# Depthwise-separable 1x1 convolution: the weight load in two parts, the first input chunk on a second queue, fewer filler matmuls, and the last wait moved to GpSimd

One core of one Trainium2 chip. The metric is the device time of one execution in microseconds (us), as the median of repeated runs; the kernel before takes 574.88 us (three runs, 574.85 to 574.94).

## The reference

```python
H = W = 384; C = 384; k = 1            # x: (1, 384, 384, 384), dw: (1, 1, 384), pw: (384, 384), bf16
out = x * dw[0, 0]                     # k = 1: the depthwise step is a scale per channel
return jnp.einsum('bhwc,cd->bhwd', out, pw)
```

So it is one matrix product of 147456 rows with a 384x384 matrix, whose row c is scaled by dw[c] first.

## The kernel before

The rows are worked in 288 supertiles of 512 rows. Each is loaded by SyncE, transposed by VectorE in two halves (32x32 blocks, into T), multiplied on TensorE in 48 small matmuls (four at a time, each on a quarter of the array's rows), copied out of PSUM by ScalarE and stored by SyncE. The first chunks of the input are small (1, 1, 2, 2, 4 supertiles, then 10 each): I call them x0 to x4. Each supertile waits for both halves of its T in turn, so it can start once the first half is there. Before the loop the scaled weights w_r are built: TensorE multiplies pw by scaled selection matrices, and ScalarE (five copies) and VectorE (one) bring the result to SBUF. TensorE runs filler matmuls on constants meanwhile, and repeats some build matmuls, to keep its clock up. "Lands" means that all of a load's data has arrived and its semaphore says so.

The loads at the start, and SyncE's last wait:

```python
        nc.scalar.dma_start(dw_row[:], dw.rearrange("a e c -> a (e c)")).then_inc(s_dw, 16)
        nc.sync.dma_start(pw_n[:], pw.rearrange("(k p) d -> p k d", p=P)).then_inc(s_pw, 16)
        load_x(0)
        # ... the list of further loads and stores, in order of need
        for _, f, a in sorted(todo, key=lambda a: a[0]):
            if f is store and a[0] == 0:

                for _ in range(28):
                    nc.sync.wait_ge(s_pw, 16)
            f(*a)
        for o in range(NR):
            n = sum(n_parts[t] for t, c in enumerate(chunks) if c[0] % NR == o)
            nc.sync.wait_ge(s_o[o], 16 * n)
```

The first part of TensorE's program (cut):

```python
        idle_work(4)

        nc.tensor.wait_ge(s_dw, 16)
        for k in range(3):
            mm = nc.tensor.matmul(
                PS[1][:, 0, D + k : D + k + 1],
                lhsT=dw_row[:, P * k : P * k + P],
                rhs=ones[0:1, 0:1],
                start=True,
                stop=True,
            )
        mm.then_inc(s_df)
        idle_work(4)
        nc.tensor.wait_ge(s_pw, 16)
        times = {(1, 1): 3, (2, 0): 2}
        for k in range(3):
            nc.tensor.wait_ge(s_sw, k + 1)
            for r in range(2):
                if k == 2:
                    nc.tensor.wait_ge(*w_done[r])

                for v in [0, 1] * times.get((k, r), 1):
                    mm = nc.tensor.matmul(
                        PS[(k + 1) % 2][:, 2 * r + v, :D],
                        lhsT=sel_w[64 * v : 64 * v + 64, k, r, :, :].rearrange("p q w -> p (q w)"),
                        rhs=pw_n[64 * v : 64 * v + 64, k, :],
                        start=True,
                        stop=True,
                        tile_position=(64 * v, 0),
                    )
```

The supertile (cut), with the blocks b of 64 input channels in order 0 to 5:

```python
        steps = [(b, par) for b in range(4) for par in range(2)] + [(4, 0), (5, 0), (4, 1), (5, 1)]
        # per step and quarter q: wait for T's half at b = 0 and b = 3, a matmul into PS[s][:, q],
        # and at ((2, 1), (5, 1)) a semaphore that lets VectorE overwrite that half of T
```

ScalarE's and VectorE's copies of the built weights:

```python
        def w_out(i):
            e, k, r = w_eng[i], i // 2, i % 2
            out, in_ = w_r[:, 2 * k : 2 * k + 2, r, :], w_ps(i)
            o = nc.vector.tensor_copy(out, in_) if e == 0 else nc.scalar.copy(out, in_)
            o._wait_ge(s_w, i + 1)
            o.then_inc(s_wr[e])
```

## Time and profile before

| | before |
|---|---|
| time, median | 574.88 us (574.85 to 574.94) |
| span of the profiled run | 573.1 us |
| TensorE, loop matmuls | 561.8 us busy, 0.2 us idle |
| first build matmul / first loop matmul | 3.98 / 7.06 us |
| last stores landed | 572.0 us |

By this reading only what lies before 7.06 and behind the last matmul (568.85) can change with such an edit. The prediction below shows the lines and how to read them.

### The profile page before, as it was taken

How to read it: one execution, taken by the hardware profiler on the slowest of the kernel's cores; microseconds unless marked ns; L12 is line 12 of the kernel's file. 1: busy time of each engine (PE TensorE's matmuls, PEld its weight loads, DVE VectorE, ACT ScalarE, POOL GpSimd, SP SyncE). 2: the span in 40 equal slices, each digit the busy share in tenths (PEclk: the TensorE clock that was granted, in tenths of full speed). 3: DMA queues.
4: the chain of work that ended last, by engine and by line, in shares of the span. 5: the costliest groups of instructions: out<-in, count | busy, mean ns of one | idle time of the engine just before them, and what ended most of it. 6: DMA issues, size and time to landing. Idle time of an engine off the chain costs nothing.

```text
span 573.1 us, 29723 instructions
## 1 busy us (share of the span) xinstructions
PE 567.5 (99%) x13877; PEld 415.5 (72%) x13877; DVE 507.7 (89%) x584; ACT 419.4 (73%) x297; POOL 0.5 (0%) x5
## 2 busy tenths in 40 slices
PE   9999999999999999999999999999999999999996
PEld 5777777777777777777777777777777777777774
DVE  7888898898898899889889889988988988988995
ACT  6777777777777777777777777777777777777775
POOL 0000000000000000000000000000000000000000
PEclk9999999999999999999999999999999999999999
DMA  8999999999999999999999999999999999999676
GB/s 332 430 350 437 418 422 434 442 415 424 428 421 419 381 400 434 398 381 400 427 390 394 392 427 392 414 402 429 390 399 430 397 393 399 424 398 380 263 286 245
DMA packets 26452, 226.88 MB, mean 396 GB/s; under 512 B 1225, under 2 KB 6986, under 8 KB 22602
## 3 DMA queue, kind: packets, MB, share of 16 engines
q1 hardware_dynamic: 25408, 226.01, 97.3%
q10 hardware_dynamic: 1034, 0.79, 0.4%
q14 instruction: 9, 0.07, 0.0%
q8 instruction: 1, 0.02, 0.0%
HBM read 113.54 MB, written 113.25 MB: 396 GB/s over the span
## 4 chain that ended last, share of the span: by engine, by line
PE 98%; DMA 0%; ACT 0%; issue 0%; DVE 0%; DVEq 0%
PE ps L191 97%; PE ps L208 0%; DMA out_dram<-O 0%; PE ps L239 0%; ACT O L326 0%; ACT w_r L289 0%; DVE O L324 0%; DVEq L102 0%; PE ps L221 0%
## 5 line engine op out<-in xcount | busy, mean ns | idle before, releaser
L191 PE MATMUL ps<-w_r,T 32*128 32x384 bf16 x13824 | 561.8, 321 | 0.2 <-ACT w_r L289 0.2
L276 DVE STREAM_TRANSPOSE T<-X 128x384 uint32<-128x384 uint32 x572 | 500.9, 878 | 55.3 <-DMA X<-in_x_dram 0.8
L191 PEld LDWEIGHTS ps<-w_r,T 32*128 32x128 bf16 x13824 | 413.1, 93 | 149.1 <-issue 0.7
L326 ACT CAST O<-ps 128x1536 bf16<-128x1536 f32 x287 | 413.3, 1440 | 146.8 <-PE ps L191 146.8
L289 ACT CAST w_r<-ps 128x768 bf16<-128x768 f32 x5 | 3.7, 805 | 1.5 <-PE ps L239 1.4
L208 PE MATMUL ps<-const-bfloat16-1.0 32*128 32x384 bf16 x32 | 2.8, 516 | 1.1 <-PEq L348 1.1
L276 DVE STREAM_TRANSPOSE T<-Xl 128x384 uint32<-128x384 uint32 x4 | 3.5, 878 | 0.4
L324 DVE CAST O<-ps 128x384 bf16<-128x384 f32 x2 | 1.0, 553 | 3.1 <-DMA out_dram<-O 3.1
L239 PE MATMUL ps<-pw_n,sel_w 64*128 64x384 bf16 x18 | 2.9, 507 | 0.0
L239 PEld LDWEIGHTS ps<-pw_n,sel_w 64*128 64x128 bf16 x18 | 1.2, 139 | 1.9 <-issue 1.2
L264 ACT ACT_TABLE_LOAD x1 | 1.3, 1283 | 1.5 <-POOLq L102 1.5
L208 PEld LDWEIGHTS ps<-const-bfloat16-1.0 32*128 32x128 bf16 x32 | 1.1, 124 | 1.6 <-issue 1.4
L289 DVE CAST w_r<-ps 128x768 bf16<-128x768 f32 x1 | 1.0, 958 | 1.1 <-PE ps L239 1.1
L294 DVE TENSOR_REDUCE sel<-eye 128x64 f32<-128x128 bf16 x1 | 0.3, 289 | 1.5 <-POOL eye L254 1.5
L323 ACT CAST O<-ps 128x384 bf16<-128x384 f32 x2 | 0.9, 482 | 0.5 <-PE ps L191 0.5
L301 DVE COPY dw_f<-ps 128x3 f32<-128x3 f32 x1 | 0.2, 161 | 0.9 <-PE ps L221 0.9
L304 DVE TENSOR_SCALAR sel_w<-sel,dw_f 128x256 bf16<-128x256 f32 x3 | 0.9, 349 | 0.0
L221 PEld LDWEIGHTS ps<-const-bfloat16-1.0,dw_row 1*128 1x128 bf16 x3 | 0.3, 115 | 0.4 <-DMA dw_row<-in_dw_dram 0.4
L264 ACT COPY warm<-const-float32-0.0 128x1 f32<-128x1 f32 x2 | 0.3, 190 | 0.0
L254 POOL TENSOR_SCALAR_AFFINE_SELECT eye<-const-bfloat16-1.0 128x128 bf16<-128x128 bf16 x1 | 0.3, 294 | 0.6 <-POOLq L102 0.6
L221 PE MATMUL ps<-const-bfloat16-1.0,dw_row 1*128 1x1 bf16 x3 | 0.3, 176 | 0.0
L348 POOL MEMSET const-uint8-127<- 128x1 uint8 x1 | 0.1, 103 | 0.0
(3 smaller groups left out, 0.3 us busy)
## 6 DMA issues: line engine op xcount, KB each, us to landing
X<-in_x_dram SPq DMA_DIRECT2D x26, 3840.0 KB, 21.9
out_dram<-O SPq DMA_DIRECT2D x26, 3840.0 KB, 27.7
X<-in_x_dram SPq DMA_DIRECT2D x3, 1536.0 KB, 17.8
out_dram<-O SPq DMA_DIRECT2D x4, 768.0 KB, 9.5
out_dram<-O SPq DMA_DIRECT2D x2, 1536.0 KB, 15.1
X<-in_x_dram SPq DMA_DIRECT2D x3, 768.0 KB, 8.1
X<-in_x_dram SPq DMA_DIRECT2D x1, 2304.0 KB, 19.4
out_dram<-O SPq DMA_DIRECT2D x1, 2304.0 KB, 11.2
```

Source lines behind the costliest of these rows:

```text
L191: mm = nc.tensor.matmul(PS[s][:, q, :D], lhsT=Ts[s][32 * q : 32 * q + 32, b, par::2], rhs=w_r[32 * q : 32 * q + 32, b, par, :], start=(b, ...
L208: nc.tensor.matmul(PS[0][:, 2 * (i % 2) + i // 2, :D], lhsT=ones[32 * i : 32 * i + 32, 0:P], rhs=ones[32 * i : 32 * i + 32, :], start=True ...
L221: mm = nc.tensor.matmul(PS[1][:, 0, D + k : D + k + 1], lhsT=dw_row[:, P * k : P * k + P], rhs=ones[0:1, 0:1], start=True, stop=True,)
L239: mm = nc.tensor.matmul(PS[(k + 1) % 2][:, 2 * r + v, :D], lhsT=sel_w[64 * v : 64 * v + 64, k, r, :, :].rearrange("p q w -> p (q w)"), rhs ...
L254: nc.gpsimd.affine_select(out=eye[:], in_=ones[:, 0:P], pattern=[[-1, P]], compare_op=mybir.AluOpType.is_equal, fill=0.0, base=0, channel_ ...
L264: nc.scalar.copy(warm[:, s : s + 1], nc.const_aps.tensor(0.0, [P, 1], F32)).then_inc(s_a[s])
L276: ins = nc.vector.transpose(out=Tw[:, 3 * h : 3 * h + 3], in_=Xw[:, :, j, 96 * h : 96 * h + 96].rearrange("p k (b w) -> p b k w", w=32),)
L289: o = nc.vector.tensor_copy(out, in_) if e == 0 else nc.scalar.copy(out, in_)
L304: nc.vector.tensor_scalar_mul(sel_w[:, k], sel[:].unsqueeze(2).to_broadcast([P, 2, 4, 32]), dw_f[:, k : k + 1]).then_inc(s_sw)
L323: nc.scalar.copy(Ov[:, q, j, :], PS[s][:, q, :D]).then_inc(s_a[s])
L324: nc.vector.tensor_copy(Ov[:, q + 1, j, :], PS[s][:, q + 1, :D]).then_inc(s_d)
L326: a = nc.scalar.copy(Ov[:, :, j, :], PS[s][:, :, :D])
```

## The change

Its intent is to start the loop sooner. The first two thirds of pw come in one load with runs of 1536 bytes instead of 768, which puts even rows of pw in one slot and odd rows in the next; so the selection matrices, the dw slices and the copies go by the parity of the row (blocks 0 and 2, then 1 and 3), and the loop takes its blocks in the order 0, 2, 1, 3. The last third is a second load. x0 goes out on ScalarE's queue. Eight fillers fewer stand before the build, and the repeated build matmuls move from the second step to the third. The wait for the last stores passes from SyncE to GpSimd.

```diff
--- before.py
+++ after.py
@@ -68,7 +68,7 @@
 
     pw_n = consts.tile([P, 3, D], BF16, name="pw_n")
     eye = consts.tile([P, P], BF16, name="eye")
-    sel = consts.tile([P, 2, 32], F32, name="sel")
+    sel = consts.tile([P, 2, 2, 32], F32, name="sel")
     sel_w = consts.tile([P, 3, 2, 4, 32], BF16, name="sel_w")
     w_r = consts.tile([P, NB, 2, D], BF16, name="w_r")
     dw_row = consts.tile([1, C], BF16, name="dw_row")
@@ -92,6 +92,7 @@
     s_o = [nc.alloc_semaphore(f"s_o{i}") for i in range(NR)]
     s_dw = nc.alloc_semaphore("s_dw")
     s_pw = nc.alloc_semaphore("s_pw")
+    s_pw2 = nc.alloc_semaphore("s_pw2")
     s_df = nc.alloc_semaphore("s_df")
     s_sw = nc.alloc_semaphore("s_sw")
     s_dwf = nc.alloc_semaphore("s_dwf")
@@ -146,8 +147,12 @@
 
 
         nc.scalar.dma_start(dw_row[:], dw.rearrange("a e c -> a (e c)")).then_inc(s_dw, 16)
-        nc.sync.dma_start(pw_n[:], pw.rearrange("(k p) d -> p k d", p=P)).then_inc(s_pw, 16)
-        load_x(0)
+        load_x(0, nc.scalar)
+        nc.sync.dma_start(
+            pw_n[:, 0:2].rearrange("p t d -> p (t d)"),
+            pw[0 : 2 * P, :].rearrange("(p t) d -> p (t d)", t=2),
+        ).then_inc(s_pw, 16)
+        nc.sync.dma_start(pw_n[:, 2], pw[2 * P : C, :]).then_inc(s_pw2, 16)
 
         todo = []
         for t, (g, i, off, first, L) in enumerate(chunks):
@@ -161,9 +166,6 @@
                 for _ in range(28):
                     nc.sync.wait_ge(s_pw, 16)
             f(*a)
-        for o in range(NR):
-            n = sum(n_parts[t] for t, c in enumerate(chunks) if c[0] % NR == o)
-            nc.sync.wait_ge(s_o[o], 16 * n)
 
 
 
@@ -178,7 +180,7 @@
             return PS[0 if i in (2, 3) else 1][:, 2 * (i % 2) : 2 * (i % 2) + 2, :D]
 
 
-        steps = [(b, par) for b in range(4) for par in range(2)] + [(4, 0), (5, 0), (4, 1), (5, 1)]
+        steps = [(b, par) for b in (0, 2, 1, 3) for par in range(2)] + [(4, 0), (5, 0), (4, 1), (5, 1)]
 
         def supertile(s, rv):
             for b, par in steps:
@@ -198,7 +200,7 @@
                     )
                     if (b, par) == steps[0] and q == 0:
                         mm._wait_ge(s_a[s], rv)
-                    if (b, par) in ((2, 1), (5, 1)) and q == 3:
+                    if (b, par) in ((1, 1), (5, 1)) and q == 3:
                         mm.then_inc(s_pe)
 
 
@@ -220,26 +222,30 @@
         for k in range(3):
             mm = nc.tensor.matmul(
                 PS[1][:, 0, D + k : D + k + 1],
-                lhsT=dw_row[:, P * k : P * k + P],
+                lhsT=dw_row[:, 2 * P :] if k == 2 else dw_row[:, k : 2 * P : 2],
                 rhs=ones[0:1, 0:1],
                 start=True,
                 stop=True,
             )
         mm.then_inc(s_df)
-        idle_work(4)
+        idle_work(2)
         nc.tensor.wait_ge(s_pw, 16)
-        times = {(1, 1): 3, (2, 0): 2}
+        times = {(2, 0): 3, (2, 1): 2}
         for k in range(3):
-            nc.tensor.wait_ge(s_sw, k + 1)
             for r in range(2):
+                if k == 0:
+                    nc.tensor.wait_ge(s_sw, r + 1)
                 if k == 2:
+                    if r == 0:
+                        nc.tensor.wait_ge(s_pw2, 16)
+                        nc.tensor.wait_ge(s_sw, 3)
                     nc.tensor.wait_ge(*w_done[r])
-
+                slot, h = (r, k) if k < 2 else (2, r)
                 for v in [0, 1] * times.get((k, r), 1):
                     mm = nc.tensor.matmul(
                         PS[(k + 1) % 2][:, 2 * r + v, :D],
-                        lhsT=sel_w[64 * v : 64 * v + 64, k, r, :, :].rearrange("p q w -> p (q w)"),
-                        rhs=pw_n[64 * v : 64 * v + 64, k, :],
+                        lhsT=sel_w[64 * v : 64 * v + 64, slot, h, :, :].rearrange("p q w -> p (q w)"),
+                        rhs=pw_n[64 * v : 64 * v + 64, slot, :],
                         start=True,
                         stop=True,
                         tile_position=(64 * v, 0),
@@ -262,6 +268,10 @@
         ).then_inc(s_sel)
         for s in range(2):
             nc.scalar.copy(warm[:, s : s + 1], nc.const_aps.tensor(0.0, [P, 1], F32)).then_inc(s_a[s])
+
+        for o in sorted(range(NR), key=lambda o: (o - len(groups)) % NR):
+            n = sum(n_parts[t] for t, c in enumerate(chunks) if c[0] % NR == o)
+            nc.gpsimd.wait_ge(s_o[o], 16 * n)
 
         def transposes(t, j):
             g, i, off, first, L = chunks[t]
@@ -285,24 +295,25 @@
 
         def w_out(i):
             e, k, r = w_eng[i], i // 2, i % 2
-            out, in_ = w_r[:, 2 * k : 2 * k + 2, r, :], w_ps(i)
+            out, in_ = (w_r[:, k : k + 3 : 2, r, :] if k < 2 else w_r[:, 4:6, r, :]), w_ps(i)
             o = nc.vector.tensor_copy(out, in_) if e == 0 else nc.scalar.copy(out, in_)
             o._wait_ge(s_w, i + 1)
             o.then_inc(s_wr[e])
 
         nc.vector.wait_ge(s_sel, 1)
-        nc.vector.tensor_reduce(
-            out=sel[:],
-            in_=eye[:].rearrange("p (v w r) -> p r w v", v=2, r=2),
-            op=mybir.AluOpType.add,
-            axis=mybir.AxisListType.X,
-        ).then_inc(s_dwf)
+        for k, split in enumerate(("p (v h w) -> p h w v", "p (v w h) -> p h w v")):
+            nc.vector.tensor_reduce(
+                out=sel[:, k],
+                in_=eye[:].rearrange(split, v=2, h=2),
+                op=mybir.AluOpType.add,
+                axis=mybir.AxisListType.X,
+            ).then_inc(s_dwf)
         nc.vector.wait_ge(s_df, 1)
         nc.vector.tensor_copy(dw_f[:], PS[1][:, 0, D : D + 3]).then_inc(s_dwf)
-        nc.vector.wait_ge(s_dwf, 2)
+        nc.vector.wait_ge(s_dwf, 3)
         for k in range(3):
             nc.vector.tensor_scalar_mul(
-                sel_w[:, k], sel[:].unsqueeze(2).to_broadcast([P, 2, 4, 32]), dw_f[:, k : k + 1]
+                sel_w[:, k], sel[:, k // 2].unsqueeze(2).to_broadcast([P, 2, 4, 32]), dw_f[:, k : k + 1]
             ).then_inc(s_sw)
         for i in range(6):
             w_out(i)
```

## The prediction

> **What bounds the kernel now.** I read the groups of instructions first, then the chain of work that ended last cut to the first 22 us, then the timeline of the same stretch and of the last 7 us, and last the transfers.
>
> Of the groups, one row is the kernel:
>
> ```profile
> L191 PE MATMUL ps<-w_r,T 32*128 32x384 bf16 x13824 | 561.8, 321 | 0.2 <-ACT w_r L289 0.2
> L326 ACT CAST O<-ps 128x1536 bf16<-128x1536 f32 x287 | 413.3, 1440 | 146.8 <-PE ps L191 146.8
> ```
>
> The loop's 13824 matmuls keep TensorE busy 561.8 us with 0.2 us of idle time; ScalarE waits 146.8 us for TensorE, not the other way. They run four at a time: 13824/4 = 3456 rounds, 561.8/3456 = 162.6 ns a round. For 384 columns that is the floor of the warm array (next part). The change touches nothing that the loop repeats: the same 48 matmuls for each of 288 supertiles of 512 rows, in another order of blocks, and the semaphore that frees half of T still fires after the third block. So the 561.8 us stay, and the time is
>
> start of the first loop matmul + 561.8 + what follows the last matmul.
>
> The chain of the head says what sets that start:
>
> ```profile
> 2.63 1.30 PE ps L208 x13
> 3.93 0.04 issue
> 3.98 2.12 PE ps L239 x12
> 6.10 0.02 issue
> 6.12 0.81 ACT w_r L289
> 6.93 0.14 issue
> 7.06 14.94 PE ps L191 x361
> ```
>
> L208 is filler on constants, L239 builds the scaled weights, L289 copies them to SBUF. The chain blames the filler for the start at 3.98. The timeline and the rows of the tile pw_n put another cause beside it:
>
> ```profile
> 0.96 0.43 SPq L149 DMA_DIRECT2D pw_n<-in_pw_dram  x1
> 3.98 2.93 PE L239 MATMUL ps<-pw_n,sel_w 64*128 64x384 bf16 x18
> 4.52 3.80 ACT L289 CAST w_r<-ps 128x768 bf16<-128x768 f32 x5 [1.43 <-PE ps L239]
> DMA to landing us min/median/max: 3.0/3.0/3.0
> ```
>
> pw is issued at 0.96 and lands 3.0 us later, at about 3.95. Filler and pw end together, so only removing both moves the build. From the build's first matmul (call it t0 = 3.98) the rest is fixed work: 0.54 us to ScalarE's first copy (4.52), then copies that stand end to end. The loop needs the first three of ScalarE's: 4.52 + 3 x 0.80 = 6.92, and it starts at 7.06. So **loop start = t0 + 3.08**.
>
> The tail, from the timeline and the queue's waits:
>
> ```profile
> 569.55 0.85 SPq L142 DMA_DIRECT2D out_dram<-O  x2
> SPq L166 <- DMA out_dram<-O: 1.6, 1, 1.6
> ```
>
> The last matmul ends near 568.85, the last stores are issued by 570.40, SyncE waits 1.6 us for them (to 572.0), and the span ends at 573.1: 1.1 us of leaving the program. The time (574.88) is 1.8 us more than the span.
>
> **What the Trainium skill says.**
> 1. "TensorE: Matmul & The Clock Gate", section "Back-to-back issue gap": a warm matmul of N columns follows the last after about N/2.4 + 2.5 ns. For N = 384: 162.5. The trace agrees, 162.6.
> 2. Same page, "Part 1: The HAM clock gate": the array runs at half rate until one activity window of about 3.4 us was busy, and the windows run free. The trace agrees in part. Filler and build matmuls show 516 and 507 ns on average against 321 in the loop; pairs of the build stand 0.32 us apart = 384/1.2. Only the last pair (394 ns, at 6.51) is shortened, so the clock rose at about 6.6 us, just before the loop, although the page's clock row says full throughout. At the end the slice 573.25 to 573.50 shows 0.52 on average, i.e. a drop at about 573.26: 166 windows of 3.413 us (the page's 4096 cycles) back from there is 6.65. Estimate: the deciding window of this run was 3.23 to 6.65.
> 3. "DMA: Bandwidth & Descriptors", section "Queues, rings and completion order": each DMA engine alternates between the issuers' queues packet by packet. "Issuing engines are not separate DMA queues" adds that a second issuer saves issue time only. The trace before has pw and x0 on one queue, so it doesn't show that.
>
> **The change part by part.**
>
> *pw in two loads.* The first is 192 KB in 128 runs of 1536 bytes instead of 288 KB in 384 runs of 768 bytes. The DMA rates in half microseconds before:
>
> ```profile
> 2.00:2.50 0.50, 0.50 (x15) 0.22 (x10) 0.00 (x0) 0.50 (x1) 0.00 (x0) 1.00 0.52 103
> 2.50:3.00 0.50, 0.50 (x15) 0.32 (x11) 0.29 (x2) 0.49 (x3) 0.00 (x0) 1.00 1.05 335
> 3.00:3.50 0.50, 0.50 (x12) 0.22 (x4) 0.50 (x3) 0.09 (x1) 0.00 (x0) 1.00 1.13 421
> ```
>
> The last column is GB/s. pw's 295 kB: 51 by 2.5, 167 more by 3.0, the last 77 at 421 GB/s by 3.18; it counts as landed 0.77 us later. The first load, 197 kB: if it has the engines alone from 2.5 at 335 GB/s, 51 + 146 is there at 2.94, landed at 3.71. If longer runs double the slow start (103 by 2.5, 94 left), 2.78 and 3.55. If x0's transfer, now on another queue and issued at about 1.5 (its data from about 2.55), takes half of the rate from 2.5 on: 51 + 84 by 3.0, 62 left at 210, 3.29, landed 4.06, nothing gained. I take **3.70**, between the first and a mixture of the others: gain 0.25 us.
>
> *Fewer fillers.* Eight matmuls fewer are two rounds of 0.32 us: filler is out of the way by about 3.2 instead of 3.93. Alone worth nothing (pw lands at 3.95); with the earlier pw it lets the build follow it. It leaves TensorE idle some 0.5 us before the build.
>
> *Copies by row parity.* The build computes the same 18 matmuls (2+2+2+2+6+4 against 2+2+2+6+4+2), the six copies keep their sizes and engines, so 3.08 us stay. VectorE makes one more reduction (0.29 us, done by 2.1, beside its wait for dw_f until 2.67): hidden. The scaled selectors end at 3.22, 3.48 and 3.75 as before; the first two are wanted at t0 and t0 + 0.32: not binding. The third build step now waits for the first ScalarE copy (t0 + 1.34), then five pairs of 0.32 end at t0 + 3.0: just not binding. The second part of pw (about 4.4) is wanted at t0 + 1.4 = 5.1.
>
> *x0 on ScalarE's queue.* One more issue of 0.47 us there moves the activation table load (1.28 us) and the two warm copies from 1.51-3.09 to about 2.0-3.6, ahead of the first copy (t0 + 0.54 = 4.3): hidden. x0 landed 3.4 us after its issue (4.9), is first read after VectorE's own copy (5.72 before, 5.45 now): hidden either way.
>
> *GpSimd waits for the stores.* SyncE's wait (to 572.0) passes to GpSimd, which holds the end of the block anyway. SyncE's leaving is then hidden, but GpSimd's leaving, and the other engines' answers to it, now come after the stores. Estimate 0.05 us saved, give or take 0.1.
>
> Sum: head -0.25, tail -0.05, clock +0.1 (next part): 574.88 - 0.2 = 574.7; the likeliest single outcome, without clock trouble, is 574.6.
>
> **The rivals.**
> - *The clock rises late.* With idle time from 3.2 to t0, the window 3.23 to 6.65 is only some 85% busy instead of all but full. The window before it, busy 62% (from 1.12), was not enough. If 85% is not enough either, the clock rises one window later, near 10.06, and 3.3 us of the loop run at half rate: +1.7 us, 576.3. Against it: four timed or profiled runs lie within 0.1 us, so the warming seems to have room. I give it 12%.
> - *x0 steals from pw.* Nothing in the head is gained and t0 stays 3.95 to 4.05: 574.9. For it: the alternation of queues that the skill tells. Against it: pw has half a microsecond of lead. 25%.
> - *The pw load shrinks more than I think*: t0 = 3.45, set then by the second selector (3.48): 574.35. 25%.
> - *Input starvation after an earlier start.* x1 landed at 7.3 and x2 at 9.2. With the loop 0.3 us earlier, supertile 1's second half of T is ready near 8.95 and wanted near 9.7; supertile 2's transposes still start at 9.27, are ready at 11.0 and wanted at 11.7. No loss unless loads slip by 0.7 us.
>
> **Range and chances.** Best case 574.2 (head -0.5, tail -0.15); middle 574.6; no gain 574.9; partly late clock 575.3; a whole window late 576.3 lies outside. Range 574.2 to 575.3. Two per cent is 11.5 us, seven times the worst of these, and head and tail together are only 11 us: within 2% is as good as sure.
>
> **What would show it.** Loop matmuls 321 ns and 561.8 us, with the first at 6.8 (6.6 to 7.1); loop start minus first build matmul 3.08; the first load of pw landed 2.75 us after issue; filler ended by 3.3 and a wait for pw of about 0.4 us; the last landing to the span's end 1.1 us. A late clock would show as loop matmuls of some 500 ns in the first microseconds and 563 us or more of busy time on the loop's row. Wrong would be: a loop row that changes by itself, a start later than 7.1 with full clock, or a time under 574.0 or over 576.5.

## The result

The changed kernel took 575.25 us (median of 6 runs, 574.88 to 575.71), the kernel before 574.80 in the same rounds (6 runs, 574.53 to 574.94). The ratio is 1.0009, with a 95% interval of 0.9996 to 1.0022; ratios here come from the mean times of the fast runs of the same rounds, so they are not quite the ratios of the medians. I had forecast a small gain (574.6); there is none, and the profiled run is 0.3 us longer.

The chain of the head in the changed kernel, to be held against that of before:

```profile
1.87 6.12 DMA X<-in_x_dram
7.99 0.02 issue
8.01 0.87 DVE T L286
8.88 0.14 issue
9.02 12.99 PE ps L193 x313
```

Where the chain of before ran from the build to the loop at 7.06, this one runs through a load of x that is issued at 1.87 and lands at 7.99, and the transpose behind it, and joins TensorE at 9.02. The timeline of the same stretch (columns: start, length, engine, line and operation, count; in brackets the idle time before and what ended it):

```profile
3.58 1.20 PE L245 MATMUL ps<-pw_n,sel_w 64*128 64x384 bf16 x8 [0.29 <-DMA pw_n<-in_pw_dram]
4.13 3.61 ACT L299 CAST w_r<-ps 128x768 bf16<-128x768 f32 x5 [0.61 <-PE ps L245]
6.47 2.13 PE L193 MATMUL ps<-w_r,T 32*128 32x384 bf16 x48 [0.36 <-ACT w_r L299]
8.01 1.56 DVE L286 STREAM_TRANSPOSE T<-X 128x384 uint32<-128x384 uint32 x2 [1.15 <-DMA X<-in_x_dram]
9.02 13.18 PE L193 MATMUL ps<-w_r,T 32*128 32x384 bf16 x320 [0.41 <-DVE T L286]
```

The build starts at 3.58 in place of 3.98, and the loop at 6.47 in place of 7.06: **0.59 us gained**, more than I had forecast. But after one supertile (48 matmuls) the loop stops and goes on at 9.02. In the kernel before, the second supertile started at 9.01: loop start 7.06 and 1.95 us of work. The loop's matmuls themselves cost nearly what they cost before (561.8 us):

```profile
L193 PE MATMUL ps<-w_r,T 32*128 32x384 bf16 x13824 | 562.0, 321 | 0.8 <-DVE T L286 0.4
```

From the second supertile on both run alike, as ScalarE's second and third copies out of PSUM show, first before, then after:

```profile
11.19 1.44 ACT L326 CAST O<-ps 128x1536 bf16<-128x1536 f32 x1 [0.51 <-PE ps L191]
13.14 1.44 ACT L326 CAST O<-ps 128x1536 bf16<-128x1536 f32 x1 [0.51 <-PE ps L191]
```

```profile
11.20 1.44 ACT L337 CAST O<-ps 128x1536 bf16<-128x1536 f32 x1 [1.11 <-PE ps L193]
13.15 1.44 ACT L337 CAST O<-ps 128x1536 bf16<-128x1536 f32 x1 [0.51 <-PE ps L193]
```

(Second supertile start = start of the second copy less 2.18; I use that for the runs below, but for e4, whose second supertile ran at half clock, the timeline.) The chunk that was waited for, x1, took this long from issue to landing, before (issued at 1.97: landed at 7.3) and after (issued at 1.87: landed at 8.0):

```profile
DMA to landing us min/median/max: 5.3/5.3/5.3
```

```profile
DMA to landing us min/median/max: 6.1/6.1/6.1
```

From x1's landing to the second supertile there are 1.03 us (a transpose of 0.87 and two hand-overs). With x1 at 7.3 it could have started at 8.3, and 0.7 us of room were left before. Now x1 comes 0.7 later and the loop 0.6 earlier. The packed trace of the changed kernel says more: x1's semaphore rises in sixteen steps, eleven of them by 6.3 and the last five between 7.7 and 8.0. So the late part of the load, not all of it, sets the 8.0.

The 0.3 us of the span come from the end. The last matmul, the last stores' issue (569.55, two of them over 0.85 us) and the last landing (572.0) stand where they stood. But SyncE's waits at the end read, in the changed kernel:

```profile
SPq L103 <- POOLq L103: 1.9, 1, 1.9
SPq L142 <- ACT O L334: 0.6, 1, 0.6
SPq L370 <- PEq L370: 0.6, 2, 0.4
SPq L370 <- POOLq L103: 0.2, 1, 0.2
```

Before, SyncE waited 1.6 us for the stores itself. Now it waits 1.9 us for GpSimd, which lets it go only after the stores have landed, and 0.2 us once more. From the last landing to the end of the span it is 1.42 us in place of 1.15.

### The profile page after: what moved, and what is told of

Read it like the earlier page. It is cut to its first block, busy times and chain, and to the rows that moved or that the text cites. A ratio compares the mean times of both kernels' runs of the same rounds, so it can differ in the third digit from the quotient of the medians.

```text
span 573.4 us, 29709 instructions
## 1 busy us (share of the span) xinstructions
PE 566.3 (99%) x13869; PEld 420.1 (73%) x13869; DVE 507.6 (89%) x585; ACT 419.0 (73%) x297; POOL 0.5 (0%) x5
## 4 chain that ended last, share of the span: by engine, by line
PE 97%; DMA 2%; DVE 0%; ACT 0%; SPq 0%; issue 0%; POOLq 0%
PE ps L193 97%; DMA X<-in_x_dram 1%; DMA out_dram<-O 0%; ACT O L337 0%; DVE O L335 0%; DVE T L286 0%; SPq L155 0%; SPq L151 0%; SPq L370 0%; POOLq L103 0%; POOLq L359 0%
## 5 line engine op out<-in xcount | busy, mean ns | idle before, releaser
L193 PE MATMUL ps<-w_r,T 32*128 32x384 bf16 x13824 | 562.0, 321 | 0.8 <-DVE T L286 0.4
L193 PEld LDWEIGHTS ps<-w_r,T 32*128 32x128 bf16 x13824 | 418.5, 93 | 144.2 <-issue 1.5
```

What stands on the lines that cost most here:

```text
L193: mm = nc.tensor.matmul(PS[s][:, q, :D], lhsT=Ts[s][32 * q : 32 * q + 32, b, par::2], rhs=w_r[32 * q : 32 * q + 32, b, par, :], start=(b, ...
```

## The experiments

Sixteen runs, in five groups of kernels that shared a chip. S stands for the changed kernel with the wait for the stores put back on SyncE (e1). "Rest" is the time from the last landing to the end of the span. Medians and lowest to highest are of the timed runs; before's median is of the same rounds. There is one profile of each kernel, so its loop start and landings are those of one execution. The diffs below are cut to the lines that matter, and are made on S unless the text says otherwise.

| run | loop starts | x1 landed | 2nd supertile | rest | profiled span | median (range) | before | ratio, 95% interval |
|---|---|---|---|---|---|---|---|---|
| before | 7.06 | 7.3 | 9.01 | 1.15 | 573.1 | | | |
| after | 6.47 | 8.0 | 9.02 | 1.42 | 573.4 | 575.25 (574.88-575.71) | 574.80 | 1.0009, 0.9996-1.0022 |
| e0 after again | 6.81 | 8.0 | 9.04 | 1.42 | 573.4 | 575.25 (574.91-575.94) | 574.87 | 1.0008, 0.9994-1.0022 |
| e1 = S | 6.44 | 8.0 | 8.99 | 1.15 | 573.1 | 574.95 (574.28-576.30) | 574.87 | 1.0008, 0.9994-1.0022 |
| e2 before, GpSimd waits | 6.89 | 7.3 | 8.84 | 1.42 | 573.2 | 575.00 (574.88-575.46) | 574.87 | 1.0003, 0.9990-1.0017 |
| e3 after, x0 on SyncE | 7.49 | 7.5 | 9.44 | 1.42 | 573.8 | 575.30 (575.02-575.77) | 574.87 | 1.0007, 0.9993-1.0021 |
| e4 S, x1 on ScalarE | 6.96 | 11.0 | 12.0 | 1.15 | 577.8 | 579.25 (577.51-580.54) | 574.84 | 1.0074, 1.0059-1.0088 |
| e5 S, old fillers | 6.76 | 7.4 | 8.71 | 1.15 | 572.9 | 575.16 (574.60-575.36) | 574.84 | 1.0005, 0.9992-1.0018 |
| e6 before, x0 on ScalarE | 7.09 | 6.1 | 9.04 | 1.15 | 573.2 | 574.79 (574.58-579.21) | 574.84 | 1.0012, 0.9988-1.0036 |
| e7 S, small load third | 6.36 | 8.7 | 9.70 | 1.15 | 573.8 | 575.60 (574.88-576.00) | 574.84 | 1.0011, 0.9998-1.0024 |
| e8 S, pair on ScalarE | 7.04 | (pair) 6.1 | 8.99 | 1.15 | 573.1 | 574.87 (574.67-575.99) | 574.79 | 1.0006, 0.9993-1.0019 |
| e9 S, pw's rest by GpSimd | 9.69 | 5.6 | 13.5 | 1.2 | 577.8 | 578.42 (577.90-579.51) | 574.79 | 1.0064, 1.0051-1.0077 |
| e10 S, x1 before pw's rest | 8.45 | 6.3 | 11.3 | 1.15 | 575.4 | 576.70 (574.91-579.49) | 574.79 | 1.0032, 1.0011-1.0053 |
| e11 S, pw's rest on ScalarE | 6.42 | 7.4 | 8.45 | 1.15 | 572.6 | 574.99 (574.29-576.16) | 574.75 | 1.0007, 0.9993-1.0021 |
| e12 as e11, pair | 8.98 | (pair) 7.0 | 12.7 | 1.15 | 576.8 | 577.21 (575.11-578.50) | 574.75 | 1.0030, 1.0016-1.0044 |
| e13 S, x0 twice (wrong) | 6.68 | 7.7, not waited for | 8.63 | 1.15 | 573.2 | 574.87 (574.78-576.70) | 574.75 | 1.0012, 0.9996-1.0027 |
| e14 before, repeats late | 6.75 | 7.8 | 8.85 | 1.15 | 573.0 | 574.72 (574.46-574.88) | 574.85 | 0.9998, 0.9984-1.0011 |
| e15 = e11 again | 6.61 | 7.5 | 8.57 | 1.15 | 572.7 | 574.83 (574.45-576.80) | 574.85 | 1.0008, 0.9994-1.0021 |

The kernel before never took over 575.5 us in the 49 runs of these rounds. Of the 40 runs of the changed kernel, e0, e1, e5, e8, e11, e13 and e15, which all split pw and use ScalarE's queue for one of the first loads, seven took 575.9 or more. So the changed head also spreads the time, and a median of five runs says little about 0.3 us.

### The end: e1 and e2 (and e0, the changed kernel again)

e0 is unaltered.

> The changed kernel again, unaltered, for its spread and a second profile. The theory (call it starvation): the loop starts near 6.5 us, 0.6 earlier than before, but x1 lands near 8.0, so that the second supertile waits about 0.6 us and starts at 9.0 as before; and the way out after the last landing takes 1.4 us in place of 1.1. So 0.3 to 0.5 us slower than before. Rival (clock): the time moves with the moment at which the clock rises, which differs from run to run; then a second profile with the clock rising later than 4.4 us would be slower by half of what falls into the loop.

It came out as the first time: x1 at 8.0, second supertile at 9.04, 1.42 us at the end. Its clock rose later: its build matmuls take 516 ns each on average, against 376 in the first profile, so its loop started at 6.81 (the cold repeats kept TensorE until then). The span was the same, so the clock is not what lost the time.

e1 puts the last wait back, e2 moves it in the kernel before:

```diff
 # e1, on the changed kernel                  # e2, on the kernel before: the reverse
+        nc.sync.wait_ge(s_o[o], 16 * n)      -        nc.sync.wait_ge(s_o[o], 16 * n)
-        nc.gpsimd.wait_ge(s_o[o], 16 * n)    +        nc.gpsimd.wait_ge(s_o[o], 16 * n)
```

> The changed kernel with the wait for the stores back on SyncE. If GpSimd's wait costs 0.27 us (last landing to end of span 1.15 before, 1.42 after), this is 0.27 us faster than the changed kernel, within 0.15 us of before, and the stretch from last landing to end is 1.15 again. If the end has nothing to do with it, it stays at 1.42 and the time at that of the changed kernel.

> The kernel before with that one part of the change alone. If the wait on GpSimd is the cost: 0.27 us slower than before, 1.42 us from last landing to end, all else as before (loop start 7.06, second supertile 9.01). If it is an interaction with the other parts: no slower.

The rest of the span follows the wait in both directions: 1.15 and 1.42 us. e1's profiled span is that of before (573.1). SyncE's waits at the end show the two states, e1 first, then e2:

```profile
SPq L171 <- DMA out_dram<-O: 1.6, 1, 1.6
```

```profile
SPq L102 <- POOLq L102: 1.9, 1, 1.9
```

So the wait on GpSimd costs 0.27 us. In e2 the profiled span rose by 0.1 us only, because the loop also started 0.17 us earlier (6.89); the reason comes with e14. Its median rose by 0.13 us (575.00 against 574.87). The timed runs alone would not have shown 0.27 us: e1's spread is 2 us.

### What the early loop start is worth: e5 and e13

e5 puts the old fillers back in S:

```diff
-        idle_work(2)
+        idle_work(4)
```

> The changed kernel with the stores' wait on SyncE and the old number of fillers. The build then starts near 3.9 in place of 3.5 and the loop at 6.9 to 7.1. Starvation theory: nothing changes behind that, since x1 lands at 8.0 and the second supertile starts at 9.0 all the same: the time of e1 within 0.1 us. Rival (the early start is worth its 0.4 us and the loss is elsewhere): 0.4 us slower than e1.

The build started at 3.87. The time (575.16) is within the spread of e1 (574.95), which is too wide to decide between 0 and 0.4 us. The profile was not what I expected: with the very same loads as e1, x1 landed at 7.4, and the second supertile started at 8.71. So x1's landing is not fixed by the order of the loads: it varies from run to run.

e13 gives the second supertile x0's rows, so that nobody waits for x1 there. Its output is wrong, which doesn't matter for the time.

```diff
+            X, sem, n = x_of(0 if t == 1 else t)      # in the transposes
+                    if t == 2: nc.vector.wait_ge(s_x[0][1], 16)
```

> Wrong result on purpose. e1 with the second supertile's transposes reading x0's rows, so that nobody waits for x1 there (x1's landing is waited for at the third). Theory: the second supertile starts 1.95 us behind the first, near 8.4, but x2 lands at 9.8, so that the third starts near 10.9 as before; the time is that of e1 within 0.1 us. It is the whole input stream, not x1 alone, that pins the head. If x1 alone were the bound, the third supertile would start near 10.4 and the time fall by 0.5 us.

The second supertile followed at once (8.63), and the third at 10.63, 0.3 us earlier than before: x2 had landed at 9.6 here. The gain lived until the eleventh supertile, the first of x5, the sixth chunk, which landed at 25.5. ScalarE's copies out of PSUM:

```profile
26.46 1.44 ACT L339 CAST O<-ps 128x1536 bf16<-128x1536 f32 x1 [0.51 <-PE ps L196]
28.75 1.44 ACT L339 CAST O<-ps 128x1536 bf16<-128x1536 f32 x1 [0.85 <-PE ps L196]
30.70 1.44 ACT L339 CAST O<-ps 128x1536 bf16<-128x1536 f32 x1 [0.51 <-PE ps L196]
```

Between the first two lies 2.29 us in place of 1.95, and the waits of that stretch name it:

```profile
DVE T L288 <- DMA X<-in_x_dram: 2.2, 1, 2.2
```

The time was that of e1, as I expected, but not by way of x2, which I had named. And x5 landed a microsecond later here (25.5) than in the kernel before (24.5) or in e11 (24.3), where an early start was kept; in e1 it landed at 25.5 too. So e13 shows that an early start can be lost at a later chunk, not that it must be. That the input stream as a whole pins the head is not shown.

### Why x1 is late: e3, e4, e6, e7, e9, e10

e3 undoes the queue part alone (x0 behind both parts of pw on SyncE's queue):

```diff
-        load_x(0, nc.scalar)
         nc.sync.dma_start(pw_n[:, 2], ...).then_inc(s_pw2, 16)
+        load_x(0)
```

> The changed kernel with x0 back on SyncE's queue behind both parts of pw. If the split of x0 and x1 over two queues is what makes x1 late (they share each DMA engine, so x1 no longer runs behind x0 but beside it, and its slowest engine ends last): x1 lands near 7.3 as before, the loop starts at 6.5 to 6.6, the second supertile at 8.5, and the time is 0.4 to 0.6 us below the changed kernel's. If x1 is late for another reason (an engine that stalls in these microseconds whatever the queue): x1 near 8.0 and the time as the changed kernel's.

x1 did land at 7.5, but now x0 was late (6.5 in place of 4.9), the loop waited for it and started at 7.49. The delay had moved to another transfer. In before, after and e3 it was the third transfer of SyncE's queue that was slow. The next five were made to test that.

e4 puts x1 on ScalarE's queue behind x0:

```diff
         load_x(0, nc.scalar)
+        load_x(1, nc.scalar)
```

> The changed kernel with the stores' wait on SyncE and with x1 issued on ScalarE's queue right behind x0. In all profiles so far the third transfer of SyncE's queue was the slow one (x1 before, after and in e1; x0 in e3, where it was third). If it is the place in SyncE's queue: x1 is now free of it and lands before 7.0, x2 becomes third on SyncE's queue and keeps near 9.8; the loop starts at 6.5 to 6.9, the second supertile no longer waits for x1 (8.4 to 8.9), and the third, which x2 then binds, starts near 10.8: 0.15 us before the kernel before, 0.6 at most. If x1 is slow wherever it is issued: lands near 8.0, the second supertile at 9.0, the time of e1.

It was far worse: x1 landed at 11.0, later even than x2 (9.9). So leaving SyncE's queue does not free x1; counting dw it was now the third transfer of ScalarE's queue. TensorE, whose first supertile had already run in part at half clock (3.05 us for 48 matmuls in place of 2.13), then stood for two microseconds, and its clock fell back. The profile by stretches (columns: busy us of TensorE, its weight loads, VectorE, ScalarE and GpSimd, with instructions; clock; DMA share; GB/s):

```profile
8.00:10.00 2.00, 2.00 (x40) 0.87 (x32) 0.00 (x0) 0.00 (x0) 0.00 (x0) 1.00 1.04 432
10.00:12.00 2.00, 0.01 (x4) 0.03 (x1) 1.00 (x2) 1.44 (x1) 0.00 (x0) 1.00 1.06 450
12.30:14.30 2.00, 2.00 (x33) 1.23 (x25) 1.99 (x4) 0.00 (x0) 0.00 (x0) 0.50 1.03 439
```

e6 moves x0 to ScalarE's queue in the kernel before:

```diff
+        load_x(0, nc.scalar)
         nc.sync.dma_start(pw_n[:], ...).then_inc(s_pw, 16)
-        load_x(0)
```

> The kernel before with x0 alone moved to ScalarE's queue; pw stays one load, so that x1 is the second transfer of SyncE's queue. If the split of x0 and x1 over two queues makes x1 late: x1 near 8.0 here too, second supertile 9.0. If it is the third place in SyncE's queue: x1 lands before 7.0 and x2 (third) is the slow one. Either way the loop starts at 7.06 as before, and the time is that of before within 0.15 us.

x1, now second on SyncE's queue, landed at 6.1 and the median didn't move, as expected (one of the six runs took 579.21, which is not explained): in this profile this part of the change is neutral by itself, and the queue split alone does not make x1 late. The DMA rates tell more. From 4 to 6 us (two slices each; the last column is GB/s), before, after and e6:

```profile
4.00:5.00 1.00, 1.00 (x8) 0.49 (x10) 0.16 (x1) 0.48 (x1) 0.00 (x0) 1.00 0.89 243
5.00:6.00 1.00, 1.00 (x10) 0.49 (x8) 1.00 (x2) 1.00 (x2) 0.00 (x0) 1.00 0.86 203
```

```profile
4.00:5.00 1.00, 0.78 (x8) 0.18 (x4) 0.55 (x1) 0.87 (x2) 0.00 (x0) 1.00 0.88 197
5.00:6.00 1.00, 0.87 (x10) 0.41 (x10) 1.00 (x2) 1.00 (x2) 0.00 (x0) 1.00 0.91 264
```

```profile
4.00:5.00 1.00, 0.98 (x8) 0.47 (x10) 0.11 (x1) 0.43 (x1) 0.00 (x0) 1.00 1.03 402
5.00:6.00 1.00, 1.00 (x10) 0.48 (x8) 1.00 (x2) 1.00 (x2) 0.00 (x0) 1.00 1.08 439
```

In the first two the transfers run at about half rate for two microseconds; in e6 they don't. In the packed trace single packets are what is slow: the 3072-byte packets, most of which take 0.12 us, took up to 0.98 us there before and 1.17 us after, and 0.34 us at most in e6. So the kernel before has the hold-up too. It hid it in the room between x1's landing and the second supertile.

e7 puts a useless load of 32 KB third on SyncE's queue in S:

```diff
         nc.sync.dma_start(pw_n[:, 2], ...).then_inc(s_pw2, 16)
+        nc.sync.dma_start(scr[:], pw[0:P, 0:P]).then_inc(s_scr, 16)
```

> The changed kernel with the stores' wait on SyncE and one more load of 32 KB, of no use, as third on SyncE's queue; x1 is fourth and issued 0.45 us later. If whatever comes third is held up for a fixed time, x1 behind it lands at about 8 to 8.4 still. If it is the bytes or the place of x1 in HBM: x1 8.4 or later. If only the transfer in third place is slowed and the queue goes on beside it: x1 lands earlier, near 7.

Those 32 KB took 4.5 us to land (6.34), and x1 behind them came at 8.7, so the second supertile started at 9.70. That so small a load was held up speaks for a hold-up that does not depend on the bytes and is handed on to what stands behind, the first of the three outcomes; but x1's 8.7 lies outside the 8 to 8.4 that I gave for it and fits "8.4 or later". So e7 does not decide between the two.

e9 has GpSimd issue the rest of pw, and e10 puts x1 ahead of it on SyncE's queue:

```diff
 # e9                                                 # e10
-        nc.sync.dma_start(pw_n[:, 2], ...)           +        load_x(1)
+        nc.gpsimd.dma_start(pw_n[:, 2], ...)                  nc.sync.dma_start(pw_n[:, 2], ...)
```

> The changed kernel with the stores' wait on SyncE and with the second part of pw issued by GpSimd, so that x1 is second on SyncE's queue, as in e6 where nothing was held up. If the third place is what delays x1: x1 lands before 6.5 and x2 before 9.2; loop start 6.4 to 6.8, second supertile 1.95 later; 0.4 to 0.6 us faster than before, unless pw's second part lands after 5.5 by this way. If x1 is late because x0 runs beside it on another queue while pw is split: x1 near 8.0, time of e1.

> The changed kernel with the stores' wait on SyncE and x1 ahead of the second part of pw on SyncE's queue. If the third place delays: now pw's second part is late (5 to 6.5 for its slowest engine, against 3.4 to 3.9 for most in e1), x1 before 6.5; the third build step waits for pw and the loop starts at 6.8 to 8, with the second supertile 1.95 behind it. If x1 is late by itself: x1 near 8.0 and pw's second part before 4.5, loop start 6.5.

In both, x1 as second landed early (5.6 and 6.3), and the rest of pw, third or by GpSimd, late (7.9 and 6.7). The build waited for it, as TensorE's timeline of e9 and of e10 shows:

```profile
7.98 1.78 PE L247 MATMUL ps<-pw_n,sel_w 64*128 64x384 bf16 x10 [2.69 <-DMA pw_n<-in_pw_dram]
```

```profile
6.74 1.78 PE L249 MATMUL ps<-pw_n,sel_w 64*128 64x384 bf16 x10 [1.83 <-DMA pw_n<-in_pw_dram]
```

The loop started at 9.69 and 8.45, part of it with a cold clock (loop matmuls busy 563.7 and 562.7 us in place of 561.9): slower by 3.6 and 1.9 us. That x1 was early and pw late in e10 agrees with the third place; but x0, second on ScalarE's queue, was late there as well (6.5). And in e6 SyncE's third transfer, x2, was not slow (7.9, in place of 9.2 before). So the place in the queue is a tendency, not the law. What holds the DMA engines up stays open.

### Can the early start be kept: e8, e11, e12, e15

e8 makes x0 and x1 one load of two supertiles, on ScalarE's queue:

```diff
-    head, tail = [[1, 1, 2, 2, 4]], [[6, 4], [4, 2, 1, 1]]
+    head, tail = [[2, 2, 2, 4]], [[6, 4], [4, 2, 1, 1]]
```

> The changed kernel with the stores' wait on SyncE and with the input's first two chunks (one supertile each) made one load of two supertiles, on ScalarE's queue; so the second supertile's input no longer comes third on SyncE's queue. Starvation theory: the pair lands by 5.5, the loop starts near 6.5 and the second supertile follows 1.95 us later, at 8.4 to 8.5; the third is then bound by the next chunk (third on SyncE's queue, landing 8.5 to 9.8), starting at 10.4 to 10.8: 0.2 to 0.6 us faster than before. Rival (the loss sits in something else that pins the pipeline at 9.0): second supertile at 9.0, time of before.

The pair landed at 6.06, not by 5.5, so now the loop itself waited for it (start 7.04); the second supertile followed after 1.95 us. Time and span are those of before. The early start was lost in the first supertile instead of the second.

e11 keeps x0, x1 and x2 behind one another on SyncE's queue, x0 right behind pw's first part; pw's rest goes to ScalarE's. e12 does the same with the pair.

```diff
-        load_x(0, nc.scalar)
+        nc.scalar.dma_start(pw_n[:, 2], pw[2 * P : C, :]).then_inc(s_pw2, 16)
         nc.sync.dma_start(pw_n[:, 0:2] ...).then_inc(s_pw, 16)
-        nc.sync.dma_start(pw_n[:, 2], pw[2 * P : C, :]).then_inc(s_pw2, 16)
+        load_x(0)
```

> The changed kernel with the stores' wait on SyncE, pw's second part on ScalarE's queue and x0 back on SyncE's, second behind pw's first part. x0, x1, x2 then come one behind the other on one queue, as before. If that order of the input is what matters: x0 lands near 4.6, x1 near 7.3 and x2 near 9.2 as before, the loop starts near 6.5, the second supertile 8.4 to 8.5, the third near 10.4: 0.5 us faster than before. If a hold-up of about a microsecond per DMA engine hits the third transfer anyway and its length varies: x1 between 6.5 and 8, and the gain between 0.6 and 0.

> As e11, and the first two chunks as one load of two supertiles, so that only two transfers are needed before the third supertile. The pair lands near 5.4 to 5.6 (1.9 us of data at 400 GB/s from about 2.9), the loop starts at 6.5 to 6.7, the second supertile follows 1.95 us later, the third waits for the next chunk if that lands after 9.2. 0.4 to 0.6 us faster than before if the pair isn't held up; the same as before if it lands near 6.1 as in e8.

e11's profile is what the change had been meant to be: x0 at 4.7, x1 at 7.4, loop start 6.42, second supertile 8.45. The first supertiles' copies:

```profile
8.60 1.44 ACT L337 CAST O<-ps 128x1536 bf16<-128x1536 f32 x1 [0.92 <-PE ps L196]
10.63 1.44 ACT L337 CAST O<-ps 128x1536 bf16<-128x1536 f32 x1 [0.59 <-PE ps L196]
12.58 1.44 ACT L337 CAST O<-ps 128x1536 bf16<-128x1536 f32 x1 [0.51 <-PE ps L196]
```

The span was 572.6, and that run took 574.35. But of the five runs two took 575.20 and 576.16, so the median is no better. e12 fell to the other side: even pw's first part landed at 4.3, the rest at 7.2, and all was late. e11 was run once more, as e15.

> e11 again, the best order of loads so far, for its spread: e11 had runs from 574.29 to 576.16. If the length of the hold-up per DMA engine is what spreads it: again some runs near 574.3 and some at 575 and above, and the profile's time follows from x1 and x2: second supertile at x1's landing + 1.03 or 1.95 behind the first, whichever is later. If e11's slow runs were noise: all near 574.3, clearly faster than before.

Again a gain in the profile (572.7) and a median equal to before (574.83 against 574.85), with one run at 576.80. e11 ends earlier when the DMA engines go well; it does not beat the kernel before over the runs.

### Where the build became shorter: e14

```diff
-        times = {(1, 1): 3, (2, 0): 2}
+        times = {(2, 0): 3, (2, 1): 2}
```

> The kernel before with one part of the change alone: the repeated build matmuls moved from the second step to the third. In the profile of before ScalarE's third copy starts at 6.12, 0.91 us behind the second, because the repeats keep its step until 6.07; without them copies start 0.69 apart. If that is where 0.2 us of the earlier loop start came from: loop start minus first build matmul 2.89 in place of 3.08, so 6.87; the input (x1 at 7.3) has room, so the second supertile starts at 8.8, and the time falls by 0.2 us where the clock rises after about 5.5 us (where it rises earlier, before has 2.9 too). Rival: 3.08 is the copies' own length; then 7.06 and no change.

From the first build matmul (3.87) to the loop it took 2.88 us, as expected, in place of 3.08. (Where the clock rose only after the build, the move costs time instead: e0 and e13 took 3.20 and 3.19 us, held by the five cold pairs of the third step.) x1 landed at 7.8 in this run, with the same loads as before: the second supertile started at 8.85, so not all of the gain was passed on. The median is 0.13 us below before, within the noise.

## Why the prediction was wrong

- **"The 561.8 us stay": right.** The loop's row reads 562.0 us in the changed kernel at 321 ns a matmul. What was wrong is that the loop keeps going once started; see the starvation point.
- **pw's first part: right, and better than forecast, but not for the reason given.** I took its landing at 3.70; it landed at 3.54. That is my lowest estimate (3.55, from a slow start at twice the rate), but the rate from 2.0 to 2.5 us was 104 GB/s against 103 before. By my own sum the data were then complete near 2.93, and landed 0.6 us later, not 0.77. x0 on the other queue cost it nothing that shows (with x0 behind it on SyncE's queue, in e3, it landed at 3.47). The build started 0.40 us earlier, not 0.25.
- **"So loop start = t0 + 3.08" and "3.08 us stay": wrong by 0.19, in the favourable direction.** It was 2.89. I read ScalarE's five copies, 3.80 us in one merged line, as standing end to end at 0.80. They start 0.69 apart, since each begins before the last has ended; the Trainium skill says so under "Perfetto Trace Analysis", section "Optimizing Scalar/DVE Operations" (the write acknowledgement overlaps with the next instruction), and this trace agrees: 4.13, then 5.51 for the third. In the kernel before, the third started at 6.12, because it waited for a build step whose matmuls were repeated. The chain had shown it: L239 until 6.10, then one copy. The change moves the repeats behind that step, and I counted 18 matmuls in both and stopped there. e14 shows the term alone: 2.88. An early clock does the same, since the repeats then end sooner (e2: 2.90). The changed kernel's profile had both (its build matmuls took 323 ns from 4.45 on), so there the gain was in part luck; in e0, with a late clock, my "just not binding" failed and it was 3.20.
- **"Input starvation ... No loss unless loads slip by 0.7 us": this is the first of two steps that failed.** It stood as a rival without a share of the chances, and its own condition came true: x1 slipped from 7.3 to 8.0, the loop came 0.59 us forward, and the second supertile started at 9.02 as before. The head's gain was 0, not 0.25 us. I had taken the landing times of before as fixed while the change reordered those very loads. The 0.7 us were misread as well: I took them from the second half of T (ready 8.95, wanted 9.7), but a supertile starts with the first half. With the loop at my own 6.81 the second supertile would start at 8.76, and x1, 1.03 us ahead of that, had to land by 7.73: 0.45 us of room behind 7.28. The rates of before (243 and 203 GB/s from 4 to 6 us, after 421 from 3 to 3.5) had shown a hold-up that nothing in the program explained; I saw it and did not ask what it would hit next. What is shown: the wait for x1 (the chain), that it isn't the clock (e0), that with x1's wait taken away the second and third supertiles start earlier (e13; the gain was lost to x5 in that run), and that a profile with x1 at 7.4 keeps the gain (e11). That the change makes x1 later is not shown as surely: with its loads x1 landed at 8.0, 8.0, 8.0, 7.4, 7.7 (after, e0, e1, e5, e13), with those of before at 7.3, 7.3, 7.8 (before, e2, e14).
- **"GpSimd waits ... 0.05 us saved, give or take 0.1": wrong in sign, the second step that failed.** It costs 0.27 us (e1, e2), outside the margin; as an error of 0.32 us it is larger than the head's 0.25. I had seen that "the other engines' answers" would now come after the stores, but priced that round trip at about what SyncE's own leaving cost.
- **"x0 was first read after VectorE's own copy ... hidden either way": right, by luck.** x0 landed at 5.28 in place of the 4.9 I took; its transposes started at 5.32, 0.04 us later. In e10 it landed at 6.5 by the same queue, and VectorE waited 1.24 us for it.
- **The late clock: its worst case did not occur.** In the changed kernel's two profiles the build matmuls were warm at the end or the clock rose as the loop began, in spite of the idle 0.3 us. In e9, e10 and e12, where the build stood still for 1.5 to 2.7 us, the clock did come late, at a cost of 0.8 to 1.8 us in the loop's row (562.7 to 563.7 in place of 561.9). In e4, with no such stand in the build, part of the first supertile ran cold too. So the rival was real, though not in those two profiles.
- **The sum.** Forecast: head -0.25, end -0.05, clock +0.1 (my 12% of 1.7 us would make it 0.2). Measured in the profile: head 0.0, end +0.27, clock 0. The profiled spans differ by that 0.27. The medians differ by 0.45, and by 0.38 in e0's rounds; the remainder is within the spread of the runs and is not explained. A range that holds 575.25 came out right for the wrong reason, by way of a clock that was not late.

## What to carry to other kernels

Before pricing an earlier start, write down for each of the first few inputs when it lands and when it is wanted, and treat landings in the first microseconds as uncertain by as much as they vary between runs: here the room was 0.7 us and the change used all of it. Take the room from the part that is wanted first. A merged line of several instructions hides where they wait; look at their starts one by one. And measure which engine should hold a program's last wait: here the move from SyncE to GpSimd cost 0.27 us.

## What the Trainium skill lacked or had wrong

- No page tells of a hold-up of the DMA engines in a program's first microseconds ("DMA: Bandwidth & Descriptors" would be the place). Here the rate fell from 421 GB/s (3.0 to 3.5 us, before) to 197-264 between 4 and 6 us (before, after) and not at all in e6 (402, 439); 32 KB took 4.5 us to land (e7). It fell mostly on a queue's third transfer; its cause is open.
- "DMA: Bandwidth & Descriptors", "Issuing engines are not separate DMA queues": a second issuer is said to save only issue time. In these profiles moving a load to the other queue changed landings by more: x1 from 7.3 to 6.1 when x0 left its queue (e6; 0.5 us of that is the earlier issue), and from 8.0 to 11.0 when x1 itself moved (e4).
- "TensorE: Matmul & The Clock Gate", the table "Why this matters for your kernels", asks for no idle gaps over about 3 us. In e4 a gap of 2.0 us (10.0 to 12.0) was enough: the clock stood at 0.50 from 12.3 to 15.7.
- No page prices which engine holds a program's last wait: 1.15 us from landing to end with SyncE, 1.42 with GpSimd (e1, e2).
